# Making the parts of a head's row maxima on GpSimd and turning them in two pieces, in an attention and MLP kernel on one core

## The chip, the cores and the metric

The kernel runs on one core of one Trainium2 chip. A core has TensorE (PE; its weight loads are shown apart as PEld), VectorE (DVE), ScalarE (ACT), GpSimd (POOL) and SyncE (SP, which here only issues DMAs). Each engine works off its own instructions in order; they wait for one another through semaphores. The metric is the time of one execution on the device in microseconds, as a median over several runs.

## The reference

A block with attention and a gating MLP side by side, for one sequence of 2048 rows with 512 features; 32 heads of 16 features share one key and one value head.

```python
x = A_x
xn = _layernorm(x, axis=-1)
s = _A_ref(xn, A_wq, A_wk, A_wv, A_wo)
g = _silu(_B_ref(xn, B_w1, B_b1, B_w2))
return x + s * g
...
q = (lambda x, *d: x.transpose(*d))((x @ wq).reshape(B, S, H, Dh), 0, 2, 1, 3)
k = x @ wk
v = x @ wv
scores = jnp.einsum("bhqd,bkd->bhqk", q, k) * (Dh ** -0.5)
p = _softmax(scores, axis=-1)
o = jnp.einsum("bhqk,bkd->bhqd", p, v)
return (lambda x, *d: x.transpose(*d))(o, 0, 2, 1, 3).reshape(B, S, H * Dh) @ wo
...
h = jnp.einsum("bsd,df->bsf", x, w1) + b1
sp = jnp.log1p(jnp.exp(-jnp.abs(h))) + jnp.where(h > 0, h, jnp.zeros_like(h))  # stable softplus
act = h * jnp.tanh(sp)
return jnp.einsum("bsf,fd->bsd", act, w2)
```

`_A_ref` is the middle part and `_B_ref` the last; F, the MLP's inner size, is 1792.

## The kernel before

**Tiles and passes.** The 2048 rows are cut into four chunks of 512, and a chunk's 32 heads into eight passes with four heads each, so there are 32 passes (`NU`); the program and this text call a pass "head v", v from 0 to 31. One `qt` tile holds the four queries of a pass in two halves of the partitions (side a, rows 0 to 63 and 64 to 127) and two column blocks (p). Each pass has 16 steps, one for each block of 128 keys, 512 steps in all.

**A step.** TensorE makes four score tiles e (`score`, L1090), which ScalarE takes through the exponential into `pts` (L1095), and the value products pv of the step two before (L1176). The row maxima that the softmax subtracts are made one pass ahead: TensorE makes four products m of the next pass (`m_one`, L1118), each 128 queries against 512 keys, and VectorE reduces each to its maximum in `mb` (L1122). Beside them runs a filler: matmuls of the projections and of the MLP (`xps`, L118 and L122). Both halves of the array are used at once, one by the filler and one by e and m. Where a filler group has the right length, four steps are emitted together as a *unit* in two halves (`unit`); the last 20 steps are a *tail* without products m (`tail_pair`). PSUM has eight banks: three for e, three for m (`ps_m`, L134), one for pv and one for the filler.

**The rows of a head.** When all 64 products m of head v are reduced, `c_rows(v)` makes the two rows that are put into the query tile so that the scores come out with the maximum subtracted: `reduce` (L1141) takes the maximum over the key blocks into `mp`, `parts` (L1144, L1146) makes the rounded part of the negated maximum and the rest of it, `turn` (L1153) turns both with four transposes of 32x32 into `cr`, and `move` (L1162) sends the rows with one DMA for each side to `qt`, both from SP. In the main loop `top_rows` puts these on a queue and runs one of its entries behind each step, two behind each half of a unit, three in the tail, and none behind a step in which VectorE had a filler to evacuate (`evacs`): reduce, then parts, then turn and move.

**What sets the order.** The program is written out by hand: each engine runs its instructions in the order in which this Python code emits them. GpSimd has the elementwise work of the MLP (hb, t, u, act), the splitting of weights and activations into a rounded part and a rest (`hi_pool`, L170, and `sub`, L175), and the last steps of the normalization. `charge` adds an assumed time to a running account of GpSimd's work, which decides when later steps of the MLP are emitted.

**The lead-in.** Ahead of the main loop a list planner (L1475) emits the normalization, K and V, the first queries and the rows of head 0. It picks the task that can start earliest by assumed times. While nothing is ready TensorE gets products that nobody reads (`keep_warm`, L1431). The planner ends shortly before the time `cdone` at which the rows of head 0 are taken to have landed (L1498).

Of the kernel before, what the change touches and what calls it, by code (L numbers as in the profile page):

```python
# [14 lines left out]
F32 = mybir.dt.float32  # L15
F32R = mybir.dt.float32r
AF = mybir.ActivationFunctionType
ALU = mybir.AluOpType
AX = mybir.AxisListType

P = 128
# [12 lines left out]
LEAD = 20  # L34
# [32 lines left out]
def m_need(v):  # L67

    return 32 * (v + 1)
# [59 lines left out]
def block_kernel(ctx: ExitStack, tc: tile.TileContext, x, wq, wk, wv, wo, w1, b1, w2, out):  # L129
    nc = tc.nc  # L130
    cp = ctx.enter_context(tc.tile_pool(name="const", bufs=1))
    sb = ctx.enter_context(tc.tile_pool(name="work", bufs=2))
# [7 lines left out]
    pe, act, dve, pool, sp = nc.tensor, nc.scalar, nc.vector, nc.gpsimd, nc.sync  # L140

    step = [-10 ** 6]
    lead = {}
# [4 lines left out]
    def us_of(t):  # L148
        return base[1] + (t - base[0]) * STEP_US
# [4 lines left out]
    def charge(us):  # L154
        busy[0] = max(busy[0], us_of(step[0]) + (0 if lead else 1.5)) + us
# [3 lines left out]
    def sp_at(us):  # L159

        sp_t[0] = max(sp_t[0], us_of(step[0])) + us
        return step_of(sp_t[0] + 2.6) - 1
# [24 lines left out]
    def f(ap):  # L187
        return ap.bitcast(F32)
# [413 lines left out]
    def fill(quota, more=False):  # L602
        while quota > 0:
            if cur["g"] is None and not begin():
                return
            g = cur["g"]
            n = min(quota, len(g.mms) - cur["n"])
            for m in g.mms[cur["n"]:cur["n"] + n]:
                m(cur["ps"])
            cur["n"] += n  # L610
            quota -= n
            if finish() and not more:
                return
# [432 lines left out]
    def take(n):  # L1046
        r = [m1s.popleft() for _ in range(min(n, len(m1s)))]
        queue.extend(r)
        return r

    take(AHEAD)
    for c in range(NC):
        for k in range(3):
            a = take(2)
# [18 lines left out]
    mb_of = {}  # L1073
# [29 lines left out]
    m_next = [0, 0]  # L1103
# [30 lines left out]
    def c_rows(v):  # L1134

        mp = sb.tile([P, 2, 3, 8], F32R, tag="mp", name=f"mp{v}", bufs=2)
        mx = f(mp[:, :, 0])
        w = {}

        def reduce():  # L1140
            dve.reduce_max(out=mx, in_=mb_of[v].rearrange("p b (a z) -> p a z b", a=2), axis=AX.X)  # L1141

        def parts():
            dve.tensor_reduce(out=mp[:, :, 1], in_=mx.rearrange("p a (z o) -> p a z o", o=1), axis=AX.X,  # L1144
                              op=ALU.max, negate=True)
            dve.tensor_reduce(out=f(mp[:, :, 2]), in_=f(mp[:, :, 0:2]).rearrange("p a s z -> p a z s"), axis=AX.X,  # L1146
                              op=ALU.add, negate=True)

        def turn():
            cr = w["cr"] = sb.tile([32, P], F32, tag="cr", name=f"cr{v}", bufs=2)  # L1150
            for b in range(4):
                z = slice(32 * b, 32 * b + 32)
                dve.transpose(cr[:, z], f(mp[z, :, 1:3]).rearrange("p a s z -> p a (s z)"))  # L1153

        def move():
            q, cr = qt_of[v], w["cr"]
            if not lead:
                sp_t[0] = max(sp_t[0], us_of(step[0]) + 4.0)
            for a in range(1, -1, -1):
                r = 64 * a + 48  # L1160
                sp_at(0.68)
                sp.dma_start(f(q[r:r + 2]).rearrange("o p (t n) -> o (p t) n", n=P), cr[16 * a:16 * a + 16])  # L1162
        return reduce, parts, turn, move

    def pv(s):
# [114 lines left out]
    now = [0.0]  # L1280

    def when(t):
        now[0] = t
        step[0] = max(step[0], (t - E0) / STEP_US)
        k = min(timed, default=1)
        if k <= step[0] and busy[0] + E0 < t + 0.5 and not plan["POOL"]:
            timed[k].pop(0)()
            if not timed[k]:
                del timed[k]
# [6 lines left out]
    def task(eng, us, fn, deps=(), **kw):  # L1296
        t = Task(eng, us, fn, deps, **kw)
        plan[eng].append(t)
        return t
# [61 lines left out]
    for c in range(NC):  # L1361
        z = slice(4 * c, 4 * c + 4)
# [96 lines left out]
    def best(eng):  # L1459
        found = None  # L1460
        for k in plan[eng]:
            s = k.start(T[eng])
            if s is not None and (found is None or (max(s, T[eng] + 0.1), k.prio) < (max(found[0], T[eng] + 0.1), found[1].prio)):
                found = (s, k)
        return found
# [7 lines left out]
    cdone = [None]  # L1473
    kind = [None]
    while True:  # L1475
        opts = []
        for e in ("ACT", "DVE", "POOL", "SP"):
            if e == "POOL":
                T[e] = max(T[e], busy[0] + E0)
            if b := best(e):  # L1480
                early = max(now[0], b[1].start(0))
                opts.append((early if e == "DVE" and b[1].prio < 2 and b[0] < early + 5.0 else b[0], e, b[1]))
        b = best("PE")
        m = m_ready(T["PE"])
        if m is not None and b and b[0] < T["PE"] + 0.2 and T["DVE"] > T["PE"] + 1.0:
            m = None
        if m is not None and (b is None or m <= b[0] + 0.05 or T["DVE"] < T["PE"] + 0.3 and m <= T["PE"] + 0.1):
            opts.append((m, "PE", "M"))
        elif b:
            opts.append((b[0], "PE", b[1]))  # L1490
        e0 = min((o for o in opts if o[1] == "PE"), default=None, key=lambda o: o[0])
        low = min((o[0] for o in opts), default=None)
        if e0 is None or e0[0] > T["PE"] + 0.35:
            opts.append((T["PE"], "PE", "X"))
        if not any(o[1] == "ACT" and o[0] < T["ACT"] + 0.1 for o in opts):
            opts.append((T["ACT"], "ACT", "J"))
        s, e, k = min(opts, key=lambda o: o[0])
        if cdone[0] is not None and s >= cdone[0] - 0.4 and min(m_next) >= 2 * LEAD:  # L1498
            break
        when(s)  # L1500
        for tag in items:
            load(tag)
        if k == "M":
            d = max(T["DVE"], s + 0.45)
            for a in pick[0]:
                if m_next[a] == len(mseq):
                    mseq.append(pick[1])
                    got[pick[1][0]] += 1
                m_one(a)
                d += 0.6  # L1510
                m_ends.append(d)
            T["DVE"] = d
            T["PE"] = s + (0.25 if kind[0] == "M" else 0.45)
            kind[0] = "M"
            if vdone[0] == 0 and got[0] == 32 and m_next[0] == m_next[1]:
                vdone[0] = 1
                r = c_rows(0)
                r1 = task("DVE", 1.2, lambda: (r[0](), r[1](), r[2]()))

                def move():  # L1520
                    r[3]()
                    cdone[0] = now[0] + 2 * 0.65 + 2.0
                task("SP", 1.3, move, [r1])
        elif k == "X":
            fresh = cur["g"] is None
            if cur["g"] is not None or not waiting and (vdone[0] or begun[0] < 1 + (s - 18) / X_US) and begin():
                begun[0] += fresh
                fill(3)
                T["PE"] = s + 0.23 * 3 + (0.2 if kind[0] == "M" else 0)
                kind[0] = "X"  # L1530
            else:
                keep_warm()
                T["PE"] = s + 0.25
                kind[0] = "X"
        elif k == "J":
            tag = next((g for g in ("wq", "ws", "wb") if not any(soon(k, s) for k in plan["POOL"]) and arrived(g) and busy[0] + E0 < s + (4.5 if g == "ws" else 0.5)), None)
            n = ran[0]
            if tag:
                split(tag)
                T["ACT"] = s + 0.6  # L1540
            else:
                gap[0] = 0
                if not plan["POOL"]:
                    act_jobs(1)
                T["ACT"] = s + (0.65 if ran[0] > n else 0.15)
        else:
            plan[e].remove(k)
            if k.fill and cur["g"] is not None and s < 27.0:
                fill(1)
            elif k.fill and cur["g"] is None and not waiting:  # L1550
                keep_warm()
            k.fn()
            T[e] = max(s, T[e]) + k.us + (0.15 if e == "PE" and kind[0] == "M" else 0)
            k.end = T[e]
            if e == "PE":
                kind[0] = "T"
# [9 lines left out]
    rowq = deque()  # L1566
    skip = [0]

    def top_rows(n):
        if vdone[0] < 8 * NC and min(m_next) >= m_need(vdone[0]):  # L1570
            r = c_rows(vdone[0])
            rowq.extend([r[0], r[1], lambda r=r: (r[2](), r[3]())])
            vdone[0] += 1
        for _ in range(min(n, len(rowq))):
            rowq.popleft()()

# [176 lines left out]
```

## Time and profile before

| | before |
|---|---|
| median of 3 runs | 1565.1 us (1565.07 to 1565.53) |
| the profiled execution | 1565.04 us |
| its span, first to last instruction | 1563.2 us |
| POOL TENSOR_TENSOR on 128x512 | 1.29 us each |
| POOL TENSOR_SCALAR on 128x512 | 0.62 us each |

The page of the profile lists busy times by engine, the chain of work that ended last, and groups of equal instructions with what ended the idle time before them. A timeline row gives start, duration, engine, line, operation, what is written and read, how many instructions are merged in the row, and in brackets the engine's idle time before it with what ended it. A windows row gives a stretch, its length, each engine's busy time with the number of instructions, the granted share of TensorE's clock, and the DMA share and rate.

### The profile page before, as it was taken

How to read it: one execution, taken by the hardware profiler on the slowest of the kernel's cores; microseconds unless marked ns; L12 is line 12 of the kernel's file. 1: busy time of each engine (PE TensorE's matmuls, PEld its weight loads, DVE VectorE, ACT ScalarE, POOL GpSimd, SP SyncE). 2: the span in 40 equal slices, each digit the busy share in tenths (PEclk: the TensorE clock that was granted, in tenths of full speed). 3: DMA queues.
4: the chain of work that ended last, by engine and by line, in shares of the span. 5: the costliest groups of instructions: out<-in, count | busy, mean ns of one | idle time of the engine just before them, and what ended most of it. 6: DMA issues, size and time to landing. Idle time of an engine off the chain costs nothing.

```text
span 1563.2 us, 31137 instructions
## 1 busy us (share of the span) xinstructions
PE 1551.0 (99%) x11722; PEld 862.5 (55%) x11722; DVE 1366.9 (87%) x2376; ACT 1295.0 (83%) x2509; POOL 637.8 (41%) x668
## 2 busy tenths in 40 slices
PE   9999999999999999999999999999999999999998
PEld 6545655555455565565555556556554555565654
DVE  7988888888989988898999998898889999889945
ACT  6599888779888788877989788798798887879786
POOL 5788339437348121440543424054044232404213
PEclk9999999999999999999999999999999999999999
DMA  6343123224131313112214231222321223121021
GB/s 205 110 140 125 39 85 127 68 85 139 59 120 56 105 32 112 58 33 91 64 31 139 78 93 30 76 81 86 97 60 32 87 69 111 31 86 45 8 75 42
DMA packets 68498, 125.46 MB, mean 80 GB/s; under 512 B 15262, under 2 KB 29900, under 8 KB 68348
## 3 DMA queue, kind: packets, MB, share of 16 engines
q1 hardware_dynamic: 67916, 122.68, 24.7%
q8 instruction: 93, 1.52, 0.4%
q10 hardware_dynamic: 432, 0.79, 0.1%
q14 instruction: 57, 0.47, 0.1%
HBM read 75.57 MB, written 26.21 MB: 65 GB/s over the span
## 4 chain that ended last, share of the span: by engine, by line
PE 97%; DVE 2%; ACT 1%; DMA 0%; issue 0%; SPq 0%; DVEq 0%
PE xps L122 44%; PE pv L1176 32%; PE m L1118 11%; PE e L1090 6%; PE xps L118 1%; DVE mb L1122 1%; PE wop L122 0%; PE kp L356 0%; PE xp L315 0%; DMA pts<-in_dram 0%; ACT pts L1095 0%; PE y2ps L122 0%; PE warm L1431 0%; PE wop L118 0%; DVE cr L1153 0%
## 5 line engine op out<-in xcount | busy, mean ns | idle before, releaser
L1122 DVE TENSOR_REDUCE mb<-m 128x1 f32<-128x512 f32 x2048 | 1265.6, 682 | 152.2 <-PE m L1118 118.3
L1095 ACT ACTIVATE pts<-e 128x512 f32<-128x512 f32 x2048 | 1065.6, 605 | 220.1 <-PE e L1090 162.4
L1118 PE MATMUL m<-ks,qt 48*128 48x512 f32 (+1 forms) x2048 | 846.1, 424 | 1.7 <-DVE mb L1122 1.4
L1090 PE MATMUL e<-qt,ks 64*128 64x512 f32 x2048 | 752.1, 407 | 0.4 <-ACT pts L1095 0.4
L1176 PE MATMUL pv<-pts,vaug 128*32 128x512 f32 x4096 | 530.1, 603 | 0.0
L1118 PEld LDWEIGHTS m<-ks,qt 48*128 48x128 f32 (+1 forms) x2048 | 371.3, 185 | 91.3 <-DVE mb L1122 54.0
L1090 PEld LDWEIGHTS e<-qt,ks 64*128 64x128 f32 x2048 | 376.0, 186 | 26.7 <-ACT pts L1095 12.9
L122 PE MATMUL xps<-wbs,act 64*128 64x512 f32 x1270 | 324.0, 399 | 0.1
L122 PE MATMUL xps<-xt,ws 64*128 64x512 f32 x1128 | 312.3, 409 | 1.0 <-ACT pts L1095 1.0
L122 PEld LDWEIGHTS xps<-xt,ws 64*128 64x128 f32 x1128 | 194.3, 185 | 184.9 <-ACT pts L1095 123.2
L122 PEld LDWEIGHTS xps<-wbs,act 64*128 64x128 f32 x1270 | 227.3, 184 | 97.2 <-ACT pts L1095 26.8
L1176 PEld LDWEIGHTS pv<-pts,vaug 128*32 128x32 f32 x4096 | 88.1, 108 | 151.5 <-issue 143.9
L185 POOL TENSOR_SCALAR t<-t 128x512 f32<-128x512 f32 x56 | 34.5, 616 | 274.3 <-ACT t L814 274.3
L175 POOL TENSOR_TENSOR hb<-hb,t 128x512 f32<-128x512 f32 x56 | 72.2, 1289 | 120.7 <-ACT t L827 76.0
L122 PE MATMUL xps<-xt,wq 64*128 64x512 f32 x336 | 93.1, 409 | 0.0
L122 PEld LDWEIGHTS xps<-xt,wq 64*128 64x128 f32 x336 | 57.9, 185 | 55.0 <-ACT pts L1095 36.9
L122 PE MATMUL xps<-wbs,ot_all 64*128 64x512 f32 x288 | 79.4, 408 | 0.0
L122 PEld LDWEIGHTS xps<-wbs,ot_all 64*128 64x128 f32 x288 | 49.5, 184 | 47.1 <-ACT pts L1095 28.5
L175 POOL TENSOR_TENSOR act<-hb,act 128x512 fp32r<-128x512 f32 x56 | 72.2, 1290 | 4.7
L175 POOL TENSOR_TENSOR hb<-hb,u 128x512 f32<-128x512 f32 x56 | 72.3, 1292 | 4.4
L175 POOL TENSOR_TENSOR u<-u,t 128x512 f32<-128x512 f32 x56 | 72.0, 1286 | 4.7
L175 POOL TENSOR_TENSOR oc<-oc,sc 128x512 f32<-128x512 f32 (+1 forms) x16 | 20.6, 1288 | 113.6 <-ACT sc L1204 56.3
(164 smaller groups left out, 900.8 us busy)
## 6 DMA issues: line engine op xcount, KB each, us to landing
wbs<-w SPq DMA_DIRECT2D x39, 512.0 KB
ws<-w SPq DMA_DIRECT2D x36, 512.0 KB
qt<-qh SPq DMA_DIRECT2D x256, 32.0 KB
w<-wbs SPq DMA_DIRECT2D x14, 512.0 KB
wq<-wq SPq DMA_DIRECT2D x14, 512.0 KB
wbs<-wo SPq DMA_DIRECT2D x12, 512.0 KB
rawws<-in_dram SPq DMA_DIRECT2D x20, 256.0 KB
w<-ws SPq DMA_DIRECT2D x10, 512.0 KB
```

Of the source, the lines that this page charges most:

```text
L118: self.pe.matmul(ps, self.lhs(), self.rhs(), start=(self.k == 0), stop=(self.k == self.tot - 1))
L122: i = self.pe.matmul(ps, self.lhs()[o], self.rhs()[o], start=(self.k == 0 and self.halves == 0), stop=(self.k == self.tot - 1 and self.hal ...
L175: eng.tensor_tensor(out=o, in0=a, in1=b, op=op)
L185: pool.tensor_scalar(o, o, lim, 0.0, op0=ALU.min, op1=ALU.max)
L1090: pe.matmul(e, ks[o:o + 64, P * k:P * (k + 1)], q[o:o + 64, p], start=True, stop=True)
L1095: x = act.activation(dst, e, AF.Exp, scale=0.25)
L1118: pe.matmul(m, q[o, p, P * t:P * (t + 1)], ks[o, C * kb:C * (kb + 1)], start=True, stop=True)
L1122: return dve.reduce_max(out=mb_of[v][:, kb, z:z + 1], in_=m, axis=AX.X)
L1176: pe.matmul(o[32 * j:32 * j + 32], vaug[:, k], pt, start=(k == 0), stop=(k == 15))
```

## The change

```diff
 def reduce():
-    dve.reduce_max(out=mx, in_=mb_of[v].rearrange("p b (a z) -> p a z b", a=2), axis=AX.X)
+    dve.tensor_reduce(out=mx, in_=mb_of[v].rearrange("p b (a z) -> p a z b", a=2), axis=AX.X, op=ALU.max, negate=True)

 def parts():
-    dve.tensor_reduce(out=mp[:, :, 1], in_=mx.rearrange("p a (z o) -> p a z o", o=1), axis=AX.X,
-                      op=ALU.max, negate=True)
-    dve.tensor_reduce(out=f(mp[:, :, 2]), in_=f(mp[:, :, 0:2]).rearrange("p a s z -> p a z s"), axis=AX.X,
-                      op=ALU.add, negate=True)
-
-def turn():
-    cr = w["cr"] = sb.tile([32, P], F32, tag="cr", name=f"cr{v}", bufs=2)
-    for b in range(4):
+    if lead:
+        dve.tensor_reduce(out=mp[:, :, 1], in_=mx.rearrange("p a (z o) -> p a z o", o=1), axis=AX.X, op=ALU.max)
+        dve.tensor_tensor(out=f(mp[:, :, 2]), in0=mx, in1=f(mp[:, :, 1]), op=ALU.subtract)
+    else:
+        charge(0.5)
+        pool.tensor_scalar(mp[:, :, 1], mx, 1.0, 0.0, op0=ALU.mult, op1=ALU.add)
+        pool.tensor_tensor(out=f(mp[:, :, 2]), in0=mx, in1=f(mp[:, :, 1]), op=ALU.subtract)
+
+def turn(n):
+    if n == 0:
+        w["cr"] = sb.tile([32, P], F32, tag="cr", name=f"cr{v}", bufs=2)
+    for b in range(2 * n, 2 * n + 2):
         z = slice(32 * b, 32 * b + 32)
-        dve.transpose(cr[:, z], f(mp[z, :, 1:3]).rearrange("p a s z -> p a (s z)"))
+        dve.transpose(w["cr"][:, z], f(mp[z, :, 1:3]).rearrange("p a s z -> p a (s z)"))
...
         sp_at(0.68)
-        sp.dma_start(f(q[r:r + 2]).rearrange("o p (t n) -> o (p t) n", n=P), cr[16 * a:16 * a + 16])
+        (act if lead and a == 0 else sp).dma_start(f(q[r:r + 2]).rearrange("o p (t n) -> o (p t) n", n=P), cr[16 * a:16 * a + 16])
...
-                r1 = task("DVE", 1.2, lambda: (r[0](), r[1](), r[2]()))
+                r1 = task("DVE", 1.3, lambda: (r[0](), r[1](), r[2](0), r[2](1)))
 
                 def move():
                     r[3]()
-                    cdone[0] = now[0] + 2 * 0.65 + 2.0
-                task("SP", 1.3, move, [r1])
+                    cdone[0] = now[0] + 0.75 + 1.9
+                task("SP", 0.7, move, [r1])
...
+            elif cdone[0] is not None and s > cdone[0] - 2.5 and min(m_next) >= 2 * LEAD:
+                break
             else:
                 keep_warm()
...
 def top_rows(n):
     if vdone[0] < 8 * NC and min(m_next) >= m_need(vdone[0]):
         r = c_rows(vdone[0])
-        rowq.extend([r[0], r[1], lambda r=r: (r[2](), r[3]())])
+        r[0]()
+        r[1]()
+        rowq.extend([lambda r=r: r[2](0), lambda r=r: (r[2](1), r[3]())])
         vdone[0] += 1
+        return
     for _ in range(min(n, len(rowq))):
         rowq.popleft()()
```

The reduction over the key blocks now gives the negated maximum, so the parts are a rounding copy and a subtraction; from head 1 on GpSimd makes them. Reduce and parts go out in the step in which a head's last product is reduced, whatever VectorE has to evacuate there; two transposes follow behind the next step, and two more with the DMAs behind the one after it. In the lead-in the parts stay on VectorE, one of the two row DMAs goes out from ScalarE's queue, and the planner ends instead of adding an unread product near the end.

On VectorE, the rows of head 1 (its maxima are in `mb`, its parts `mp`, the turned rows `cr`; the reductions of head 2's products m stand between). Before:

```order
L1141 TENSOR_REDUCE mp_1457<-mb_493 128x2x8
L1122 TENSOR_REDUCE mb_1461<-m_1_0_1462 128x1
L1122 TENSOR_REDUCE mb_1461<-m_1_1_1470 128x1
L1122 TENSOR_REDUCE mb_1461<-m_1_2_1478 128x1
L1122 TENSOR_REDUCE mb_1461<-m_0_0_1485 128x1
L1144 TENSOR_REDUCE mp_1457<-mp_1457 128x2x8
L1146 TENSOR_REDUCE mp_1457<-mp_1457 128x2x8
L1122 TENSOR_REDUCE mb_1461<-m_0_1_1500 128x1
L1122 TENSOR_REDUCE mb_1461<-m_0_2_1508 128x1
L1122 TENSOR_REDUCE mb_1461<-m_0_3_1516 128x1
L1122 TENSOR_REDUCE mb_1461<-m_1_3_1523 128x1
L1153 STREAM_TRANSPOSE cr_1535<-mp_1457 32x32 x4
```

The same place with the change:

```order
L1141 TENSOR_REDUCE mp_1453<-mb_493 128x2x8
L1122 TENSOR_REDUCE mb_1459<-m_1_0_1460 128x1
L1122 TENSOR_REDUCE mb_1459<-m_1_1_1468 128x1
L1122 TENSOR_REDUCE mb_1459<-m_1_2_1476 128x1
L1122 TENSOR_REDUCE mb_1459<-m_0_0_1483 128x1
L1157 STREAM_TRANSPOSE cr_1493<-mp_1453 32x32 x2
L1122 TENSOR_REDUCE mb_1459<-m_0_1_1499 128x1
L1122 TENSOR_REDUCE mb_1459<-m_0_2_1507 128x1
L1122 TENSOR_REDUCE mb_1459<-m_0_3_1515 128x1
L1122 TENSOR_REDUCE mb_1459<-m_1_3_1522 128x1
L1157 STREAM_TRANSPOSE cr_1493<-mp_1453 32x32 x2
```

The two small reductions are gone, and the first two transposes stand in their place, one step ahead of where all four stood.

On GpSimd, the same head (hb, t and u are the MLP's tiles of a hidden block, `wbs` a weight that is split). Before:

```order
L185 TENSOR_SCALAR t_6_1444<-t_6_1444 128x512
L817 TENSOR_SCALAR u_6_1445<-t_6_1444 128x512
L175 TENSOR_TENSOR u_6_1445<-u_6_1445,t_6_1444 128x512
L175 TENSOR_TENSOR hb_6_1290<-hb_6_1290,u_6_1445 128x512
L170 TENSOR_SCALAR wbs<-rawwb_1497 128x512
L175 TENSOR_TENSOR wbs<-rawwb_1497,wbs 128x512
```

With the change:

```order
L185 TENSOR_SCALAR t_6_1440<-t_6_1440 128x512
L817 TENSOR_SCALAR u_6_1441<-t_6_1440 128x512
L175 TENSOR_TENSOR u_6_1441<-u_6_1441,t_6_1440 128x512
L175 TENSOR_TENSOR hb_6_1286<-hb_6_1286,u_6_1441 128x512
L1149 TENSOR_SCALAR mp_1453<-mp_1453 128x2x8
L1150 TENSOR_TENSOR mp_1453<-mp_1453 128x2x8
L170 TENSOR_SCALAR wbs<-rawwb_1496 128x512
L175 TENSOR_TENSOR wbs<-rawwb_1496,wbs 128x512
```

The parts of head 1 (`mp`) stand behind the four operations of one hidden block, hb with u the last of them.

On GpSimd, head 4 (qh and ql are the two parts of the queries, xt those of the normalized input). Before:

```order
L170 TENSOR_SCALAR xt_2981<-xt_2981 128x512
L175 TENSOR_TENSOR xt_2981<-xt_2981 128x512
L170 TENSOR_SCALAR qh_3_3436<-ql_3_3437 128x512
L175 TENSOR_TENSOR ql_3_3437<-ql_3_3437,qh_3_3436 128x512
L170 TENSOR_SCALAR wq_3498<-rawwq_3456 128x512
L175 TENSOR_TENSOR wq_3498<-rawwq_3456,wq_3498 128x512
```

With the change:

```order
L170 TENSOR_SCALAR xt_2977<-xt_2977 128x512
L175 TENSOR_TENSOR xt_2977<-xt_2977 128x512
L170 TENSOR_SCALAR qh_3_3432<-ql_3_3433 128x512
L175 TENSOR_TENSOR ql_3_3433<-ql_3_3433,qh_3_3432 128x512
L1149 TENSOR_SCALAR mp_3450<-mp_3450 128x2x8
L1150 TENSOR_TENSOR mp_3450<-mp_3450 128x2x8
L170 TENSOR_SCALAR wq_3497<-rawwq_3454 128x512
```

The parts of head 4 stand behind the splitting of the queries. Apart from such pairs of new rows GpSimd's order is the one of before; TensorE's lacks the two unread products at the end of the lead-in, and is otherwise the same.

## The prediction

> **What bounds the kernel now.** I read the page first (busy shares, the chain that ended last), then the groups of instructions, then windows of single steps, and last the timelines of VectorE and GpSimd around the places where a head's rows are made.
>
> ```profile
> PE 1551.0 (99%) x11722; PEld 862.5 (55%) x11722; DVE 1366.9 (87%) x2376; ACT 1295.0 (83%) x2509; POOL 637.8 (41%) x668
> PE 97%; DVE 2%; ACT 1%; DMA 0%; issue 0%; SPq 0%; DVEq 0%
> L1122 DVE TENSOR_REDUCE mb<-m 128x1 f32<-128x512 f32 x2048 | 1265.6, 682 | 152.2 <-PE m L1118 118.3
> ```
>
> TensorE is the bound: 97% of the chain is its work, and VectorE is on the chain for 2%. VectorE's own work is almost all the 2048 reductions of the products m (L1122). So what the change can win is the short waits of TensorE for VectorE; what it can lose is a new wait in VectorE's line, for TensorE has three m banks (`ps_m`, L134) and stands still at the fourth product that has not been reduced. GpSimd is busy for 41% on average, which says nothing about any one moment.
>
> Windows of the 20 plain steps in which the four transposes stand, and then of the 20 steps just ahead of them (first and last of 20, and the sum; columns: stretch, length, busy time of PE, PEld, DVE, ACT, POOL, clock, DMA):
>
> ```profile
> 116.20:119.21 3.01, 3.01 (x24) 1.39 (x22) 2.97 (x9) 2.24 (x6) 2.78 (x3) 1.00 0.00 0
> ...
> 1413.75:1416.74 2.99, 2.99 (x25) 1.41 (x23) 2.95 (x8) 2.21 (x6) 2.62 (x3) 1.00 0.00 0
> sum 60.11, PE 59.58 PEld 27.89 DVE 59.31 ACT 49.81 POOL 26.28; mean PE 2.98 PEld 1.39 DVE 2.97 ACT 2.49 POOL 1.31
> 113.36:116.20 2.84, 2.84 (x24) 1.50 (x22) 2.72 (x7) 2.06 (x6) 2.75 (x3) 1.00 0.62 234
> ...
> 1410.89:1413.75 2.86, 2.86 (x25) 1.56 (x23) 2.76 (x8) 2.59 (x7) 1.19 (x2) 1.00 0.00 0
> sum 56.87, PE 56.87 PEld 30.50 DVE 54.49 ACT 49.37 POOL 22.51; mean PE 2.84 PEld 1.52 DVE 2.72 ACT 2.47 POOL 1.13
> 162.70:168.68 5.98, 5.98 (x53) 3.80 (x48) 5.87 (x15) 4.80 (x10) 3.39 (x4) 1.00 0.24 93
> 168.68:174.66 5.98, 5.98 (x53) 3.81 (x49) 4.87 (x9) 4.13 (x8) 0.00 (x0) 1.00 0.00 0
> ```
>
> With four transposes in it VectorE fills a step (59.31 of 60.11), and the step is (60.11 - 56.87) / 20 = 0.16 us longer than the one before it, which holds the two small reductions of the parts and costs nothing. In the last two rows, half units of two steps each, the first holds parts and transposes and the second nothing of the kind: both last 5.98. There the turning is hidden.
>
> **The change part by part.** *The turning in two pieces.* A piece of two transposes is about 0.40 us by the row below; a step took the parts' reductions, nearly as much, for nothing. So the 20 plain heads lose their 0.16 each: -3.2 us. The ten heads in units have nothing to win; head 0 is made in the lead-in, and the last head's rows are made at the tail, where no product waits for them. Bounds: nothing won, to -3.2.
>
> *The parts on GpSimd.* Two small operations on 128x16 are added for each of 31 heads. The trace has no such form; the nearest are
>
> ```profile
> L1153 DVE STREAM_TRANSPOSE cr<-mp 32x32 f32<-32x32 f32 x128 | 25.4, 198 | 1.6
> L290 POOL TENSOR_TENSOR hv<-ve,rstd 128x4 f32<-128x4 f32 x3 | 0.6, 202 | 3.1 <-ACT rstd L279 3.1
> L175 POOL TENSOR_TENSOR wk<-wkv,wk 128x64 fp32r<-128x64 f32 x4 | 1.3, 322 | 0.0
> ```
>
> 0.20 for 128x4 and 0.32 for 128x64; 128x16 is nearest to the first, so I take 0.23, two of them 0.46, and with the two hand-overs 0.6 us (bounds 0.4 and 0.8). As work that is 31 x 0.6 = 19 us of an engine that is idle for 59% of the span: nothing. But VectorE's first transposes now wait for GpSimd, in order, and GpSimd does its queue in order. What counts is when GpSimd ends the operation ahead of the parts. Head 1 (the second head), GpSimd, VectorE, TensorE:
>
> ```profile
> 80.46 1.28 POOL L175 TENSOR_TENSOR hb<-hb,t 128x512 f32<-128x512 f32 x1 [5.32 <-ACT t L827]
> ...
> 118.34 1.29 POOL L175 TENSOR_TENSOR hb<-hb,u 128x512 f32<-128x512 f32 x1
> 112.05 2.48 DVE L1122 TENSOR_REDUCE mb<-m 128x1 f32<-128x512 f32 x4
> 115.86 0.39 PE L1118 MATMUL m<-ks,qt 64*128 64x512 f32 x1
> ```
>
> From 80.46 GpSimd works without a wait; the product hb with u, behind which the parts stand, ends at 119.63. VectorE reaches the place of the first two transposes at 112.05 + 2.48 = 114.53. It would wait until 119.63 + 0.6 = 120.23, transpose until 120.63, and free the first m bank at 121.31 (a reduction of 0.68). TensorE has filled its three banks and wants a fourth at 115.86: it stands still for about 5.5 us. Behind the waiting transposes stand all reductions, behind TensorE's blocked product everything, ScalarE's exponentials for want of scores too, and on SP's queue the loads and stores behind this head's row DMAs; GpSimd alone goes on. In short form: TensorE's stall = (GpSimd's end - VectorE's arrival) + 0.4, since its fourth product follows 1.3 us behind the arrival and the way back takes 0.6 + 0.4 + 0.7. Below a gap of -0.4 there is none. Head 4:
>
> ```profile
> 231.82 0.62 POOL L170 TENSOR_SCALAR wbs<-rawwb 128x512 fp32r<-128x512 f32 x1 [2.44 <-DMA rawwb<-in_dram]
> ...
> 261.00 1.29 POOL L175 TENSOR_TENSOR ql<-ql,qh 128x512 fp32r<-128x512 f32 x1
> 251.85 2.48 DVE L1122 TENSOR_REDUCE mb<-m 128x1 f32<-128x512 f32 x4
> 255.63 0.40 PE L1118 MATMUL m<-ks,qt 48*128 48x512 f32 x1
> ```
>
> 262.29 against 254.33: a gap of 7.96, a stall of 8.35 us. Again GpSimd has worked from 231.82 without a wait. The queue drew up in both places for reasons of its own: the MLP's and the splits' work of an interval comes at once.
>
> The same subtraction at heads 24, 9, 26, 7 and, just too early, 15 (for each GpSimd's row, then VectorE's):
>
> ```profile
> 1180.79 1.31 POOL L175 TENSOR_TENSOR ql<-ql,qh 128x512 fp32r<-128x512 f32 x1
> 1178.40 2.48 DVE L1122 TENSOR_REDUCE mb<-m 128x1 f32<-128x512 f32 x4
> 484.88 1.28 POOL L175 TENSOR_TENSOR xt<-xt 128x512 fp32r<-128x512 f32 x1
> 483.35 2.48 DVE L1122 TENSOR_REDUCE mb<-m 128x1 f32<-128x512 f32 x4
> 1271.31 1.28 POOL L175 TENSOR_TENSOR ql<-ql,qh 128x512 fp32r<-128x512 f32 x1
> 1270.04 2.48 DVE L1122 TENSOR_REDUCE mb<-m 128x1 f32<-128x512 f32 x4
> 393.17 1.29 POOL L175 TENSOR_TENSOR act<-hb,act 128x512 fp32r<-128x512 f32 x1
> 390.78 3.67 DVE L1122 TENSOR_REDUCE mb<-m 128x1 f32<-128x512 f32 x6
> 762.78 1.29 POOL L175 TENSOR_TENSOR act<-hb,act 128x512 fp32r<-128x512 f32 x1
> 764.77 0.16 DVE L1144 TENSOR_REDUCE mp<-mp 128x16 fp32r<-128x16 f32 x1
> ```
>
> Head 24: 1182.10 - 1180.88, a stall of 1.6. Head 9: 486.16 - 485.83, 0.7. Head 26: 0.07, 0.5. Head 7: 0.01, 0.4. Head 15: 764.07 against 764.77, a gap of -0.7, none; the others come earlier still. Together 5.5 + 8.35 + 1.6 + 0.7 + 0.5 + 0.4 = **17.0 us**. Bounds: head 1 and 4 alone with the cheaper parts, 13.4; 0.2 more at each of the six, 18.2. GpSimd in turn waits at the parts for VectorE's reduction. That holds up what stands behind them where GpSimd is early, at head 3 a split of weights:
>
> ```profile
> 200.56 0.62 POOL L170 TENSOR_SCALAR wbs<-rawwb 128x512 fp32r<-128x512 f32 x1 [10.53 <-PE m L1118]
> ```
>
> It would go out some 5 us later, behind the reduction of that head; it is a weight of the next W2 group, for which TensorE's products with W1 and Wq come first. I cost it at nothing (its cover gone, up to those 5 us). The reduction of a head that finds a late evacuation in its step now goes out at once instead of a step later (heads 7, 10, 18, 25); it needs 0.27 of VectorE either way: nothing, at most 0.2 each.
>
> *The lead-in.* Timelines of TensorE and SP:
>
> ```profile
> 76.45 0.49 PE L1431 MATMUL warm<-qt 128*128 128x512 f32 x1 [0.54 <-ACT hb L808]
> 77.00 0.49 PE L122 MATMUL xps<-xt,ws 64*128 64x512 f32 x1
> 72.54 1.43 SPq L1162 DMA_DIRECT2D qt<-cr  x2
> ```
>
> The second unread product waits for ScalarE's hb, and the first real one behind it waits for the bank. Without it the real one starts at 76.45: -0.55 us. The row DMAs were issued by 73.97, three us ahead of the first score that reads them, so sending one from ScalarE's queue gains nothing by itself; ScalarE gives 0.7 us for the issue, and its next needed work (hb behind that same TensorE group) had more room. Bounds 0 and -0.55.
>
> *The clock after a stall.* At the program's ends the trace shows what idling does to TensorE (windows, the first two of the warm-up products L1344 alone):
>
> ```profile
> 2.00:5.99 3.99, 3.99 (x9) 3.12 (x10) 1.00 0.97 331
> 6.24:9.66 3.42, 3.36 (x15) 2.44 (x13) 1.00 1.12 328
> 1558.66:1562.40 3.74, 0.00 (x0) 0.00 (x0) 1.42 (x3) 0.00 (x0) 0.67 (x1) 1.00 0.75 280
> 1562.50:1563.20 0.70, 0.00 (x0) 0.00 (x0) 0.00 (x0) 0.00 (x0) 0.00 (x0) 0.50 0.00 0
> ```
>
> The last product ends at 1558.66; 3.8 us later the granted clock is 0.50. At the start (the clock column knows no event there) nine products take 3.99 us, 0.44 each, and afterwards fifteen take 3.42, 0.23 each: half speed for 4.0 us of work. The stalls at heads 1 and 4 leave TensorE idle for some 5.4 and 8.2 us, both more than 3.8. I take a drop at both, each with 4.0 us at half speed, so 2.0 us lost: **+4.0**. Bounds 0 and twice that.
>
> The Trainium skill (TensorE: Matmul & The Clock Gate, Part 1: The HAM clock gate) says that the clock is judged in free-running windows of about 3.4 us, and halves after a window without work; the 3.8 and 4.0 us here agree. By it an idle time of 5.4 us can fall so that no whole window lies in it, which is the second case below.
>
> *Sum,* against the profiled execution's 1565.04 us (its span 1563.2; the median of three is 1565.1): 17.0 + 4.0 - 3.2 - 0.55 = +17.3, so **1582.3 us**.
>
> **The rivals.** (a) *One drop of the clock:* head 1's idle time is too short for it, head 4's is not: 1580.3. For it: 5.4 is nearer to 3.8 than 8.2 is. (b) *No drop:* 1578.3. Against it: the end of the trace. (c) *More heads caught:* the hand-overs cost 0.5 more each time, so the six stalls grow by 3 and a few heads such as 15 join with some 0.5: about 1586. Nothing in the trace prices a hand-over of VectorE to GpSimd and back with both at work. (d) *Head 4's queue keeps its old time* while everything else is some 7 us later: its stall shrinks to about 1.4 without a drop, 1573.3. Against it: that queue starts behind a DMA, and SP's queue is in order behind DMAs that wait for TensorE's and ScalarE's results, so it moves along. (e) *The other side:* GpSimd reaches the parts in time everywhere, as it does in the units: 1565.04 - 3.2 - 0.55 = 1561.3. It decides at head 1, where the product with u would have to end before 114.1, 5.5 us earlier, and at head 4 8.4 earlier; the unbroken rows ahead of both speak against that.
>
> **How the numbers follow.** Forecast 40%, (a) 20, (b) 13, (c) 9, (d) 10, (e) 8. The range 1575 to 1588 holds the first four, 82%, with the bounds of the stalls and of the clock. A measurement can tell 0.2%, 3.1 us, from no change: all but (e) are slower by more, 92%; (e) lies at -0.24%, so 5% faster and 3% within.
>
> **What would show it.** The transposes' group must show idle time released by GpSimd's mp, in a few long waits of about 5.7, 8.6 and 1.8 us, at the second, fifth and 25th head; TensorE's longest gaps must stand there and nowhere else, with windows of clock 0.50 behind the two long ones. The plain steps with transposes must last about 2.85, and the first score must come 0.55 earlier. Wrong would be: no long wait of VectorE for GpSimd at all (the queue's order is then not what holds the parts), or long waits without as long gaps on TensorE (then it has more room than three banks).

## The result and the profile after

| | before | changed |
|---|---|---|
| median, us | 1565.23 (1565.07 to 1565.53) | 1583.17 (1582.05 to 1584.33) |
| profiled execution, us | 1565.04 | 1584.33 |
| its span, us | 1563.2 | 1582.5 |

The changed kernel takes 1.0114 times as long (95% interval 1.0097 to 1.0132). The two profiled executions differ by 19.29 us, and that is what has to be explained.

The page of the changed kernel: busy time by engine, and the chain that ended last.

```profile
PE 1554.8 (98%) x11720; PEld 865.8 (55%) x11720; DVE 1359.5 (86%) x2314; ACT 1295.7 (82%) x2509; POOL 650.2 (41%) x730
PE 90%; POOL 4%; DVE 4%; ACT 1%; issue 1%; DMA 1%; POOLq 0%; SPq 0%; ACTq 0%; DVEq 0%
```

VectorE has 7 us less to do and GpSimd 12 us more, as the change means it. But GpSimd, which the line of engines on the chain did not name before, now has 4% of it: the chain leads through its queue. The waits by engine (in total, times, longest):

```profile
PEld m L1118 <- DVE mb L1122: 66.1, 110, 8.9
DVE cr L1157 <- POOL mp L1150: 18.4, 7, 8.8
PE m L1118 <- DVE mb L1122: 16.8, 11, 8.4
```

The second row is new: VectorE's transposes wait seven times for GpSimd's parts. Timelines of VectorE (its four longest waits there) and of TensorE (its gaps behind them), with the idle time ahead in brackets:

```profile
120.23 0.41 DVE L1157 STREAM_TRANSPOSE cr<-mp 32x32 f32<-32x32 f32 x2 [5.55 <-POOL mp L1150]
271.01 0.41 DVE L1157 STREAM_TRANSPOSE cr<-mp 32x32 f32<-32x32 f32 x2 [8.85 <-POOL mp L1150]
505.18 0.41 DVE L1157 STREAM_TRANSPOSE cr<-mp 32x32 f32<-32x32 f32 x2 [0.84 <-POOL mp L1150]
1200.72 0.41 DVE L1157 STREAM_TRANSPOSE cr<-mp 32x32 f32<-32x32 f32 x2 [1.69 <-POOL mp L1150]
...
121.27 0.79 PE L1118 MATMUL m<-ks,qt 64*128 64x512 f32 x1 [5.12 <-DVE mb L1122]
272.05 0.79 PE L1118 MATMUL m<-ks,qt 48*128 48x512 f32 x1 [8.42 <-DVE mb L1122]
506.22 0.49 PE L1118 MATMUL m<-ks,qt 48*128 48x512 f32 x1 [0.41 <-DVE mb L1122]
1201.76 0.50 PE L1118 MATMUL m<-ks,qt 48*128 48x512 f32 x1 [1.26 <-DVE mb L1122]
```

These are heads 1, 4, 9 and 24. Each gap of TensorE is VectorE's wait less 0.43 us. The first product behind the two long gaps takes 0.79 instead of 0.49: the clock. Windows of the changed kernel at heads 1 and 4, from the fall of the clock to its return, and two single steps, one with two transposes and one in which a head's reduction meets a late y evacuation:

```profile
120.36:127.19 6.83, 5.92 (x28) 2.68 (x32) 5.11 (x11) 2.13 (x4) 1.71 (x2) 0.50 0.15 52
267.13:277.38 10.25, 5.33 (x24) 2.62 (x24) 4.72 (x11) 2.40 (x4) 5.46 (x8) 0.50 0.03 7
1433.40:1436.25 2.85, 2.85 (x25) 1.54 (x24) 2.81 (x7) 2.06 (x5) 2.64 (x3) 1.00 0.00 0
546.76:549.94 3.18, 3.10 (x24) 1.48 (x23) 3.15 (x7) 2.38 (x6) 1.72 (x3) 1.00 0.11 40
```

5.92 and 5.33 us of TensorE's work ran at half clock. The third row is the step that lasted 2.99 in the profile before. The fourth stood at 2.88 before.

### The profile page after: what moved, and what is told of

Its sections match the earlier page's. It is cut to its first block, busy times and chain, and to the rows that moved or that the text cites. A ratio compares the mean times of both kernels' runs of the same rounds, so it can differ in the third digit from the quotient of the medians.

```text
span 1582.5 us, 31115 instructions
## 1 busy us (share of the span) xinstructions
PE 1554.8 (98%) x11720; PEld 865.8 (55%) x11720; DVE 1359.5 (86%) x2314; ACT 1295.7 (82%) x2509; POOL 650.2 (41%) x730
## 4 chain that ended last, share of the span: by engine, by line
PE 90%; POOL 4%; DVE 4%; ACT 1%; issue 1%; DMA 1%; POOLq 0%; SPq 0%; ACTq 0%; DVEq 0%
PE xps L122 42%; PE pv L1180 30%; PE m L1118 10%; PE e L1090 6%; DVE mb L1122 3%; POOL hb L175 1%; ACT pts L1095 1%; PE wop L122 0%; PE kp L356 0%; PE xps L118 0%; POOL xt L175 0%; POOL u L175 0%; PE xp L315 0%; DMA pts<-in_dram 0%; POOL ql L175 0%
```

## The experiments

**1. The parts back on VectorE**, the rest of the change kept.

```diff
-            dve.tensor_reduce(out=mx, ..., op=ALU.max, negate=True)
+            dve.reduce_max(out=mx, ...)
...
-            pool.tensor_scalar(mp[:, :, 1], mx, 1.0, 0.0, op0=ALU.mult, op1=ALU.add)
-            pool.tensor_tensor(out=f(mp[:, :, 2]), in0=mx, in1=f(mp[:, :, 1]), op=ALU.subtract)
+            dve.tensor_reduce(out=mp[:, :, 1], ..., op=ALU.max, negate=True)
+            dve.tensor_reduce(out=f(mp[:, :, 2]), ..., op=ALU.add, negate=True)
```

> Parts back on VectorE as the two small reductions of before; all else of the change kept. Theory (VectorE waits in two places for GpSimd's queue): no wait of the transposes is left, 1561.5 us (1560.5 to 1563). Rival 1 (the turning in two pieces, one step earlier, is what costs): stays above 1575. Rival 2 (three steps in a row with VectorE's extra work are more than its slack): about 1565.

Measured 1568.1 us, ratio 1.0020 (1.0011 to 1.0029). Fifteen microseconds of the loss are gone with GpSimd's parts, there is no half clock before the end and no wait at a transpose. But it is not faster than before: the expectation missed by 6.6 us. Windows of this kernel, head 8's step with reduction and parts, the step of its first two transposes, and head 7's step, which holds a y evacuation too:

```profile
435.90:438.91 3.01, 3.01 (x24) 1.43 (x23) 2.91 (x8) 2.71 (x7) 1.92 (x2) 1.00 0.66 161
438.91:441.77 2.86, 2.86 (x25) 1.56 (x23) 2.85 (x8) 2.51 (x6) 0.00 (x0) 1.00 0.49 198
389.67:393.50 3.83, 3.24 (x24) 1.56 (x22) 3.69 (x9) 3.17 (x6) 3.66 (x4) 1.00 0.02 4
```

The changed code emits reduction and parts in one step. On VectorE they are 0.27 + 0.17 + 0.19 = 0.63 us there, and the step goes to 3.01: the 0.15 won at the transposes is lost one step earlier. It is lost again in the steps with feed-forward products (5.39 for 5.12), and 0.7 us is lost where an evacuation stands in the step. The expectation had counted only the step that got shorter. The second rival named this mechanism, but at 1565 us it was 3 us short of its price.

**2 and 3. GpSimd at two heads, and at the others.** The first has GpSimd make the parts at heads 1 and 4 alone, the second at all but heads 0, 1 and 4.

```diff
...
+            if not v in (1, 4):
+                dve.tensor_reduce(out=mp[:, :, 1], ..., op=ALU.max, negate=True)
+                dve.tensor_reduce(out=f(mp[:, :, 2]), ..., op=ALU.add, negate=True)
+                return
             pool.tensor_scalar(mp[:, :, 1], mx, 1.0, 0.0, op0=ALU.mult, op1=ALU.add)
```

and in the second

```diff
-            if not v in (1, 4):
+            if not (v > 0 and v not in (1, 4)):
```

> As the first run, but the parts of heads 1 and 4 alone on GpSimd. Theory: these two make nearly all of the loss, 8.0 and 11.0 us with the clock, so the first run plus 19, about 1580.5 (1578 to 1583). Rival (GpSimd's added work costs evenly, 0.7 us for each of 31 heads, by a shared port or its hand-overs): the first run plus 1.4, about 1563.

> The changed kernel with the parts of heads 1 and 4 (and of head 0) on VectorE, the other 29 on GpSimd. Theory: 1583.2 - 18.7 - 0.3 for the lead-in, about 1564.2 (1563 to 1566). Rival (an even cost): about 1582.

Two heads: 1585.23 us, 1.0129 (1.0112 to 1.0146), 17.1 us over experiment 1. The waits view of it holds one row of this kind:

```profile
DVE cr L1162 <- POOL mp L1155: 14.0, 2, 8.5
```

TensorE's gaps are 5.12 and 8.02 us, and the trace shows half clock for 6.83 and 10.24 us, as in the changed kernel. The other 29 heads: 1565.43 us, 1.0002 (0.9992 to 1.0011), no half clock. So what separates the changed kernel from the one before stands at two heads of 32. GpSimd at the other 29 is not free: VectorE still waits 0.84 us at head 9, 1.70 at head 24 and 0.60 at head 26, and those steps are 0.66, 1.51 and 0.43 us longer than before; the 3 us that the turning wins cover that. An even price for each head falls.

**4. The turning later:** all four transposes in the second of the two steps, so that GpSimd has one step more.

```diff
-            rowq.extend([lambda r=r: r[2](0), lambda r=r: (r[2](1), r[3]())])
+            rowq.extend([lambda: None, lambda r=r: (r[2](0), r[2](1), r[3]())])
```

> The changed kernel with all four transposes in the second of the two steps, where they stood before. Theory: VectorE arrives 2.9 us later, so head 1's gap is 119.63 - 117.41 = 2.2 and its stall with two more transposes ahead 3.0, too short for the clock; head 4's 262.29 - 257.18 = 5.1, 5.9 with a drop of 2.0; heads 24, 9, 26, 7 none; each of 20 plain steps keeps its 0.16: 1565.0 - 0.3 + 3.0 + 5.9 + 2.0, about 1575.6 (1573 to 1578). Rival (the cost lies in GpSimd's part itself, wherever it is waited for): stays at 1583.

Measured 1578.34 us, 1.0085 (1.0070 to 1.0100). Waits of VectorE and gaps of TensorE at heads 1 and 4:

```profile
120.03 0.84 DVE L1157 STREAM_TRANSPOSE cr<-mp 32x32 f32<-32x32 f32 x4 [2.77 <-POOL mp L1150]
267.67 0.84 DVE L1157 STREAM_TRANSPOSE cr<-mp 32x32 f32<-32x32 f32 x4 [6.24 <-POOL mp L1150]
...
121.50 0.79 PE L1118 MATMUL m<-ks,qt 64*128 64x512 f32 x1 [2.80 <-DVE mb L1122]
269.14 0.79 PE L1118 MATMUL m<-ks,qt 48*128 48x512 f32 x1 [6.24 <-DVE mb L1122]
```

Both waits are 2.6 to 2.8 us shorter, one step's length. So the wait is an appointment: GpSimd comes when its queue lets it, and moving VectorE's side moves the wait by as much. Not expected was the clock at head 1: the gap of 2.80 is followed by 3.41 us at half clock, which hold 3.31 us of TensorE's work. That is 1.7 of the 2.7 us by which the forecast was short.

**5. Four steps on VectorE:** reduction, parts and each half of the turning in a step of its own (the four heads that start a step late keep both halves together). The parts are made on VectorE as in experiment 1.

```diff
-            r[0]()
-            r[1]()
-            rowq.extend([lambda r=r: r[2](0), lambda r=r: (r[2](1), r[3]())])
+            rowq.extend([r[0], r[1], *([lambda r=r: r[2](0)] if n else []), lambda r=r, n=n: (n or r[2](0), r[2](1), r[3]())])
             vdone[0] += 1
-            return
```

> No GpSimd part. Reduction, parts, first two transposes, last two transposes each in a step of their own on VectorE (heads 7, 10, 18 and 25, which start a step late, keep the last two together), and the change's lead-in, with the old parts. Theory (the change lost on GpSimd's queue and gained 0.15 us at each plain step that held four transposes; a reduction together with its parts is too much for one plain step, each by itself is not): no wait of VectorE at a transpose, no half clock before the end, about 20 plain steps of 3.00 become 2.85, lead-in 0.3 shorter: 1565.2 - 3.0 - 0.3 = 1561.9 us (1560.8 to 1563.2). Rival: a row that is sent one step later than before comes late for the head's first scores; TensorE then shows gaps ahead of scores at the heads, 0.5 us or more each: 1570 us or more. Rival: any split over more steps just moves the 0.15: 1565 us.

Measured 1579.14 us, 1.0084 (1.0070 to 1.0098): the rival on the rows won. Every plain step that now held two transposes did go from 3.00 to 2.85. But TensorE's waits hold a new kind:

```profile
PE e L1090 <- DMA qt<-cr: 11.0, 7, 2.0
```

Seven waits at heads 2, 13, 14, 19, 20, 22 and 28, all of them heads whose rows fall in steps with feed-forward products. One such step stands for two, so the last transposes moved some 6 us. At head 13, VectorE's last transposes, SyncE's row DMAs and TensorE's first score:

```profile
681.36 0.42 DVE L1154 STREAM_TRANSPOSE cr<-mp 32x32 f32<-32x32 f32 x2
681.80 1.36 SPq L1163 DMA_DIRECT2D qt<-cr  x2
683.89 0.47 PE L1090 MATMUL e<-qt,ks 64*128 64x512 f32 x1 [2.02 <-DMA qt<-cr]
```

**6. By head:** the four steps on VectorE at heads 0, 1, 4, 7, 9, 24, 26 and 31, GpSimd's parts at the other 24.

```diff
+            if v in (0, 1, 4, 7, 9, 24, 26, 31):
+                dve.reduce_max(out=mx, in_=mb_of[v].rearrange("p b (a z) -> p a z b", a=2), axis=AX.X)
+                return
...
+            rowq.extend([r[0], r[1], *([lambda r=r: r[2](0)] if n else []), lambda r=r, n=n: (n or r[2](0), r[2](1), r[3]())] if vdone[0] in (0, 1, 4, 7, 9, 24, 26, 31) else
+                        [lambda r=r: (r[0](), r[1]()), lambda r=r: r[2](0), lambda r=r: (r[2](1), r[3]())])
```

> As the four steps on VectorE for heads 0, 1, 4, 7, 9, 24, 26 and 31, where GpSimd was late; for the other 24 heads GpSimd makes the parts in the reduction's step, and the turning goes in two pieces over the two steps after it. Heads 10, 18 and 25 again start a step later if a late value output stands in the step. Theory (what made the change gain was the split of the turning alone; VectorE's 0.4 us of parts stood in a step that had room for them): no wait of VectorE at a transpose over 0.3 us, and the same as the four steps on VectorE within 0.7 us: 1561.6 us (1560.5 to 1563.0). Rival (each 0.4 us taken off VectorE also shortens the run): 24 heads x up to 0.1 us below the four steps on VectorE, 1559.5 us. Rival (GpSimd's two operations hold up its own queue or share the port with VectorE's reductions): above the four steps by 1 us or more.

Measured 1564.93 us, 0.9995 (0.9986 to 1.0004): no difference from before. It can't be set beside experiment 5, which met the late rows. The steps won 0.15 again, but GpSimd was late at four heads, longest at head 30:

```profile
1454.99 0.20 DVE L1162 STREAM_TRANSPOSE cr<-mp 32x32 f32<-32x32 f32 x1 [1.86 <-POOL mp L1155]
```

That one wait cost 3.2 us, since half clock followed it. In the changed kernel head 30's transposes stood in the feed-forward step after that, and did not wait. Where GpSimd is late changes with every shift of the program. Neither of the two rival effects shows: apart from the steps at GpSimd's four waits and the shortened steps, no step differs from the kernel before by more than some 0.1 us.

**7. A measured dose of delay.** As experiment 1, but at nine heads GpSimd makes the parts and repeats its first copy 4 to 27 times.

```diff
+    DOSE = {3: 18, 6: 4, 8: 7, 12: 10, 16: 14, 17: 21, 23: 27, 27: 9, 29: 5}
...
+            for _ in range(DOSE[v]):
+                pool.tensor_scalar(mp[:, :, 1], mx, 1.0, 0.0, op0=ALU.mult, op1=ALU.add)
```

> The version with reduction and parts in one step on VectorE (1568.1 us), except that at nine heads GpSimd makes the parts and repeats its copy first: 5, 4, 9, 7, 10, 18, 14, 21 and 27 extra copies at heads 29, 6, 27, 8, 12, 3, 16, 17 and 23. At 0.29 us each, less the 0 to 1.6 us by which GpSimd was early there, VectorE should wait about 0.6, 1.1, 1.8, 2.0, 2.8, 3.6, 4.0, 5.3 and 7.0 us ahead of its transposes, 28 us in all. Theory: TensorE's step grows by VectorE's wait, less up to 0.4 us at each; waits up to 2 us cost no clock; each of the five from 2.8 us on shows half clock for 3.4 to 10.2 us and 1 to 3 us of further loss: 1568.1 - 1.4 + 28 - 2 + 10 = 1603 us (1597 to 1611). Rival (the products' rows in PSUM hold TensorE's work ahead and hide a wait up to about a step): the waits to 2.8 us show less than 0.5 us each in TensorE's steps, total below 1597 us. Rival on the clock: it falls at every wait of a few tenths of a microsecond, or only over 5 us.

Measured 1593.24 us (one run). The doses came out smaller, 19.1 us of waits in all instead of 28:

```profile
1346.91 0.41 DVE L1166 STREAM_TRANSPOSE cr<-mp 32x32 f32<-32x32 f32 x2 [0.65 <-POOL mp L1159]
443.40 0.41 DVE L1166 STREAM_TRANSPOSE cr<-mp 32x32 f32<-32x32 f32 x2 [1.04 <-POOL mp L1159]
630.98 0.41 DVE L1166 STREAM_TRANSPOSE cr<-mp 32x32 f32<-32x32 f32 x2 [1.89 <-POOL mp L1159]
210.88 0.41 DVE L1166 STREAM_TRANSPOSE cr<-mp 32x32 f32<-32x32 f32 x2 [2.46 <-POOL mp L1159]
820.76 0.41 DVE L1166 STREAM_TRANSPOSE cr<-mp 32x32 f32<-32x32 f32 x2 [3.03 <-POOL mp L1159]
872.85 0.41 DVE L1166 STREAM_TRANSPOSE cr<-mp 32x32 f32<-32x32 f32 x2 [4.09 <-POOL mp L1159]
1160.96 0.41 DVE L1166 STREAM_TRANSPOSE cr<-mp 32x32 f32<-32x32 f32 x2 [5.78 <-POOL mp L1159]
```

In this order the step of the wait grew, against experiment 1, by 0.48, 0.86, 1.72, 2.28, 3.14, 4.18 and 5.89 us: the wait passes to TensorE almost whole, at every length, and no reserve hides the short ones. So far the theory holds, and the rival of the hidden waits falls. On the clock the theory fails, and both rivals with it: half clock followed the wait of 1.89 us, which was to cost none, and none followed that of 2.46, so the length of the wait does not decide it. The steps behind grew too where the clock fell: by 1.50, 2.47, 2.17 and 1.55 us behind the waits of 1.89, 3.03, 4.09 and 5.78, and by nothing behind that of 2.46. The total was below the expectation, where the rival of the hidden waits had put it, but the size of the dose explains that: 18.6 us of waits in the steps, 7.7 of clock and 1.35 won in the nine steps without parts are 24.9, beside the 25.1 that the two profiled executions differ by.

**8. The parts in two plain operations on VectorE:** four steps as in experiment 5, with a copy and a subtraction in place of the two reductions, at every head.

```diff
+            dve.tensor_scalar(mp[:, :, 1], mx, 1.0, 0.0, op0=ALU.mult, op1=ALU.add)
+            dve.tensor_tensor(out=f(mp[:, :, 2]), in0=mx, in1=f(mp[:, :, 1]), op=ALU.subtract)
```

> The four steps on VectorE, but the parts as a copy (one input) and a subtraction of two inputs, at every head. Theory (a VectorE operation with two inputs from SBUF waits for the GpSimd operation that is running and ends with it, as in the changed lead-in, where it took 1.22 us): the subtraction takes 0.25 us or less where GpSimd is idle, and 0.4 to 1.4 us where GpSimd is running, heads 1 and 4 above all; the copy never over 0.3 us; 1 to 6 us longer in all than the four steps. Rival (the 1.22 us had to do with the lead-in alone): 0.15 to 0.3 us at all heads, and the four steps' time within 0.7 us.

Measured 1584.24 us (one run), 5 us over experiment 5. Head 4, VectorE and GpSimd in this kernel:

```profile
257.29 1.20 DVE L1144 TENSOR_SCALAR mp<-mp 128x16 fp32r<-128x16 f32 x1
258.53 1.19 DVE L1145 TENSOR_TENSOR mp<-mp 128x16 f32<-128x16 f32 x1
...
257.18 1.28 POOL L175 TENSOR_TENSOR hb<-hb,u 128x512 f32<-128x512 f32 x1
258.42 1.26 POOL L175 TENSOR_TENSOR hb<-hb,t 128x512 f32<-128x512 f32 x1
```

Each operation ends as GpSimd's does, 258.49 with 258.46, and 259.72 with 259.68. With GpSimd idle both take 0.16 to 0.18 us. Of the 64 operations of the 32 heads 14 took over 0.2 us, and each of them ended 0.02 to 0.03 us behind a GpSimd operation. The copy, which has one input, waits just as the subtraction does: there the expectation was wrong. The reductions of the parts in the kernel before never do.

**9 and 10. Plain heads alone.** The four steps at the 16 heads whose rows fall in plain steps, the old three at the others, with the parts on VectorE and the lead-in of the change; and the same with both first rows on SyncE's queue.

```diff
+            if n and vdone[0] not in (2, 5, 11, 13, 14, 19, 20, 22, 28, 30, 31):
+                rowq.extend([r[0], r[1], lambda r=r: r[2](0), lambda r=r: (r[2](1), r[3]())])
+            else:
+                rowq.extend([r[0], r[1], lambda r=r: (r[2](0), r[2](1), r[3]())])
```

and in the second also

```diff
-                (act if lead and a == 0 else sp).dma_start(...)
+                sp.dma_start(...)
```

> The four steps on VectorE only at the 16 heads whose rows are made in plain steps (1, 3, 4, 6, 8, 9, 12, 15, 16, 17, 21, 23, 24, 26, 27, 29); the heads whose rows fall in steps with feed-forward products (2, 5, 11, 13, 14, 19, 20, 22, 28, 30), the last, and the four that start a step late keep the old three steps. Lead-in of the change with the old parts. Theory (the four steps lost only where a feed-forward step, twice as long, moved the last two transposes and the rows behind it, and TensorE waited 1.2 to 2 us for the rows): no gap of TensorE over 1.0 us ahead of scores, no half clock before the end, 16 x 0.15 = 2.4 us from the plain steps and 0.5 from the lead-in: 1565.6 - 2.9 = 1562.7 us (1561.6 to 1564.0). Rival (TensorE is held by something else and the 0.15 come back): 1565.2 us or more. From the lead-in's 12 products to its first products behind them 3.85 us, 4.39 before.

> The same, with both rows of the lead-in sent from SyncE's queue, as before the change. Theory (TensorE's first products wait for ScalarE's hb, not for the rows): 3.85 us there again, and the same time within 0.3 us: 1562.7 us (1561.6 to 1564.0). Rival (the second queue is what makes the lead-in shorter): 0.3 to 0.6 us longer at that place. Rival (the transfer that ScalarE issues, 0.7 to 1.25 us, holds hb up): 0.3 to 0.6 us shorter at that place.

Measured 1562.52 us, 0.9979 (0.9971 to 0.9988), and 1562.56 us, 0.9981 (0.9972 to 0.9990). No wait for rows, no half clock before the end, the 16 steps at 2.85. Both came as expected, 0.2% under the kernel before, with intervals clear of 1. The lead-in of the first, TensorE's twelve products and its first ones behind them:

```profile
72.69 3.06 PE L118 MATMUL xps<-xt,ws 128*128 128x512 f32 x12 [0.78 <-ACT hb L808]
76.53 0.50 PE L122 MATMUL xps<-xt,ws 64*128 64x512 f32 x1 [0.78 <-ACT hb L808]
```

3.84 us from one to the other. It was 4.39 before (77.00 - 72.61) and is 3.84 with one queue (76.51 - 72.67). The second queue gives nothing and costs nothing here.

## Why the prediction was right, and where it was off

The sum of the prediction beside what the two profiled executions show, step by step (a step runs from one group of eight value products to the next; the stalls are TensorE's gaps at heads 1 and 4, and at heads 7, 9, 24 and 26 what the steps grew by):

| term | predicted | measured |
|---|---|---|
| turning in two pieces, 20 plain steps | -3.2 | -3.0 |
| TensorE's stalls behind the transposes | +17.0 | +16.4 |
| clock behind them | +4.0 | +5.4 |
| lead-in | -0.55 | -0.28 |
| reductions that meet a late evacuation | 0 | +0.9 |
| two feed-forward steps that held reduction and parts | 0 | -0.4 |
| start, ahead of the change's place | 0 | +0.4 |
| sum | +17.3 | +19.4 (19.29 in all) |

**The stalls** are the mechanism forecast: the same two heads, and the waits of VectorE forecast at 5.7, 8.6 and 1.8 us were 5.55, 8.85 and 1.69. GpSimd's queue in the changed kernel, at head 1, shows why:

```profile
118.46 1.26 POOL L175 TENSOR_TENSOR hb<-hb,u 128x512 f32<-128x512 f32 x1
119.69 0.20 POOL L1149 TENSOR_SCALAR mp<-mp 128x16 fp32r<-128x16 f32 x1
119.97 0.22 POOL L1150 TENSOR_TENSOR mp<-mp 128x16 f32<-128x16 f32 x1
```

The parts run 0.50 us, and stand behind hb with u. The rule of the prediction (gap + 0.4) gave slightly too much: TensorE's gap is VectorE's wait less 0.43, which is gap + 0.1. The steps at heads 9, 24 and 26 grew by the wait less 0.18, which is nearer to the rule. Experiments 2 and 3 show that these two heads carry the loss, experiments 4 and 7 that TensorE pays VectorE's wait almost one to one.

**The clock** fell behind both, as the forecast took it, against rivals (a) and (b). Its price was undersized: the half-clock stretches held 5.92 and 5.33 us of work, so 2.96 and 2.67 lost, and not 2.0 each. By step lengths it is 2.8 and 2.6: head 1's two steps are 7.80 us longer, less the 5.12 of the gap, plus the 0.16 won by the turning; head 4's 10.89, less 8.42, plus 0.15. The threshold behind the choice, idle for more than 3.8 us, was wrong: experiments 4 to 7 have falls after gaps of 1.5 to 2.8 us. It chose rightly here, in part by luck: each of the two gaps held the whole of one of the 3.41 us windows that the last section describes (116.95 to 120.36 and 263.72 to 267.14 us, without a TensorE instruction), and for a gap of 5.12 us that depends on where it falls.

**The turning** won what was forecast. Experiments 5 and 9 show the same 0.15 without GpSimd, so it is the split and not the parts' move that wins.

**The lead-in** won half. The step that failed is the one that never looked at the new subtraction on VectorE. Timelines of VectorE and GpSimd in the changed kernel, then of ScalarE:

```profile
71.82 1.22 DVE L1146 TENSOR_TENSOR mp<-mp 128x16 f32<-128x16 f32 x1
71.74 1.27 POOL L175 TENSOR_TENSOR hb<-hb,u 128x512 f32<-128x512 f32 x1
...
73.95 1.25 ACTq L1166 DMA_DIRECT2D qt<-cr  x1
76.40 0.67 ACT L808 ACTIVATE hb<-xps,b1c 128x512 f32<-128x512 f32 x1
```

The subtraction lasted 1.22 us, until GpSimd's product ended (73.01). ScalarE issued its row 0.94 us behind the start of TensorE's twelve products, where experiment 9 issues it 0.10 ahead of it, and ScalarE's hb behind that came 0.3 us late for TensorE. The issue takes 1.25 us in both, and not the 0.7 of the prediction; without the delay this cost TensorE nothing. With the old parts and the same two queues (experiments 1 and 9) the whole 0.55 is there; with the subtraction, in experiments 4 and 8, nothing of it is (4.39 us again). That the second queue gains nothing by itself was right (experiment 10). The first score came 0.1 us later than before and not 0.55 earlier, since the twelve products themselves began 0.4 us later, the table's start; they begin at 72.40, 73.27 and 72.69 us in experiments 1, 5 and 9, whose lead-in is the same, so a difference of this size says nothing of the change.

**The late evacuations** cost more than the bound of 0.2 each: heads 10, 18 and 25 lost 0.30 each in the step of the reduction (head 7's part is among the stalls). The prediction weighed the reduction's 0.27 by itself, and not that this step then holds the evacuation too, so that VectorE is full: 3.15 of 3.18 us.

Rivals (c), (d) and (e) did not come: no further head joined but the last, whose wait of 0.64 us stands at the tail; head 4's queue moved along with the program, and GpSimd was not in time.

## What to carry to other kernels

An engine's average load says nothing about when a small operation behind its queue gets done: before work is moved to it, read when that queue comes free at each place where another engine will wait in order. Where a step is full, split the work over steps and keep it on its engine, but look at both ends of what moves: the step that receives it, and the transfer behind it, whose time to land may already be used up.

## What the runs showed of the hardware

**The clock falls on a grid, and without an idle window.** In the seven profiles with half clock in the middle of the run, every change of the clock stands a multiple of 3.41 us from the first. Most of the outcome follows from how long TensorE worked in the 3.41 us ahead of such a point. Windows of experiment 5 (no fall after the first, a fall after the second, and the stretch that follows it), and of experiment 7 (no fall, then a fall):

```profile
680.03:683.44 3.41, 1.84 (x15) 0.42 (x7) 2.29 (x5) 1.18 (x3) 2.73 (x3) 1.00 0.02 5
731.23:734.64 3.41, 1.40 (x13) 0.99 (x10) 1.17 (x3) 0.61 (x2) 0.00 (x0) 1.00 0.24 47
734.64:738.05 3.41, 3.41 (x17) 1.14 (x15) 1.51 (x3) 1.56 (x3) 0.00 (x0) 0.50 1.00 393
...
210.42:213.83 3.41, 1.92 (x14) 0.79 (x16) 2.91 (x7) 0.74 (x2) 2.20 (x4) 1.00 0.00 0
630.26:633.67 3.41, 1.94 (x16) 0.58 (x14) 2.68 (x6) 1.56 (x3) 3.07 (x6) 1.00 0.00 0
```

Two equal waits of 2.0 us, at heads 13 and 14 of experiment 5, had different ends: one lay across a border, the other wholly in one window. In these profiles every window at full clock with 1.6 us of work or less was followed by half clock, none with 2.0 us or more was, and between 1.77 and 1.97 both occurred. Busy time is not the whole rule: at the end of experiment 10 a window with 1.51 us of work (1554.55 to 1557.97, products of 128x128 alone) was followed by one at full clock, and no run here shows why. The Trainium skill (TensorE: Matmul & The Clock Gate, Part 1: The HAM clock gate) says that the windows run free and last some 3.4 us; the runs agree. It puts the fall behind a window of idling; here a window that is half idle did. Whether a short stall costs two microseconds more is thus a matter of where it falls.

**Small VectorE operations that end with GpSimd's.** In experiment 8 a copy and a subtraction of 128x16 took 0.17 us each, or up to 1.29 and 1.21 where GpSimd was in an operation. In the kernel before, the two reductions that make the parts took 0.16 to 0.19 at every head, also inside a GpSimd operation (the one at 71.42 us, while GpSimd's product ran from 71.35 to 72.62). The Trainium skill (SBUF — State Buffer, "Who interferes with whom") has the two engines share a pair of ports under an exclusive lock, which a VectorE operation with two inputs from SBUF, or a one-input operation in a two-port mode, must take; the runs agree with a lock. That these copies ran in such a mode no view shows.
